# Attention and hard-swish feed-forward on one core: bias rows on Sync, later first weights, a fixed plan of feed-forward groups

## The chip, the cores and the metric

The kernel runs on one core of one Trainium2 chip. The core has five engines with queues of their own: TensorE (PE; its weight loads are listed as PEld), VectorE (DVE), ScalarE (ACT), GpSimd (POOL) and SyncE (SP). [...] DMA transfers are issued by SP, ACT or POOL and run on 16 DMA engines. The metric is the time of one execution on the device in microseconds (us), median over runs. A profile is one further execution; its times come from that execution.

## The reference

Attention over 8 batches of 8 heads, 576 positions, head dimension 64, with a selective bias from a running sum of `s`; the heads are then put side by side into rows of 512, and a feed-forward block with a hard-swish follows.

```python
scores = scale * np.matmul(q, k.transpose(0, 1, 3, 2))
cum = np.cumsum(np.maximum(s, 0.0), axis=-1)
bias = -(cum[:, :, :, None] - cum[:, :, None, :])
scores = np.where(causal, -1000000000.0, scores + np.minimum(bias, 0.0))
attn = np.exp(scores - max) ; attn = attn / (sum + 1e-09)
x = (attn @ v).transpose(0, 2, 1, 3).reshape(4608, 512)
h = x @ w_in                       # 512 x 2048
out = (h * np.clip(h + 3.0, 0.0, 6.0) / 6.0) @ w_out   # 2048 x 512
```

## The kernel before, in words

The 64 heads are worked on in 32 pairs, p = 0 to 31; four pairs make a batch. The work of a pair stands in one pass of a loop written out by hand: scores in three parts per head and a corner (line 277 on, `scores` and `corner`), exponentials on ScalarE (line 322), masks on VectorE (line 324), the product with v (`av`, line 373), the division (`norm`, lines 395 and 396) and the transposition of the result into `xT` (line 410 and 415, later by DMA). Each engine runs its instructions strictly in the order in which the program lists them. The "slots five to eight" of the change are p = 4 to 7.

Inputs come in three ways. `load_qk` (line 103) brings q and k of one pair: for the pairs 0 to 3 and from 9 on as float32 into one of three `raw` buffers by Sync, and `cast_qk` on GpSimd makes float16 tokens of them; for the pairs 4 to 8 (the ones that are not `flat`) GpSimd issues a transfer that casts on the way, into `tok`. `load_v` brings v by Sync in three transfers, and `cast_v` on GpSimd casts it. `load_aug` (line 135) copies the bias rows of a pair, 9 KB per head, from `rows_of` in SBUF into rows 64 to 67 of one of three `qk` buffers, in two transfers. In the first batch only these rows are needed there; from p = 5 on `set_stair` also copies a stair pattern into the rows 64 to 127, and the bias rows go over it. Scores of pair p read them. The first batch's rows come out of a short chain on VectorE (`cum1` to `cum6`, lines 602 to 630).

In a pair, `get(0)` and `get(1)` prepare the transposed q and k of the next pair: on TensorE up to pair 8, from the DMA-transposed `jt` afterwards.

The weights `w_in` come in four pieces of 1 MB (`load_w_in`) and `w_out` in eight of 0.5 MB (`load_w_out`), all issued by GpSimd with a cast to float16. GpSimd thus issues, in one queue and in program order, weights, the tokens of the pairs 4 to 8 and all bias rows.

The feed-forward work is cut into groups of four matmuls: `m1(n, ft)` makes 128 of the 2048 hidden columns for a block of 512 rows, followed by one ScalarE and one VectorE instruction (lines 454 and 455), in one of two PSUM banks `ph`; `m2(n, i)` adds a quarter of one output tile of 128 rows. 9 blocks of 16 and 16 make 288 groups. From p = 4 on eight places in each pair (seven at p = 4) call `group()`, which runs one m1 or one m2 or, in an alternation of the two, nothing. `m2_ready` holds an m2 back until enough m1 are done (LAG). After the last pair the remaining groups run back to back.

Of the kernel before, what the change touches and what calls it, by code (L numbers as in the profile page):

```python
# [18 lines left out]
def kernel(  # L19
# [10 lines left out]
    nc = tc.nc  # L30
# [7 lines left out]
    NP = NHEADS // 2  # L38
    PPB = H // 2
# [60 lines left out]
    def flat(p):  # L100
        return p < PPB or p >= NPE

    def load_qk(p, i, eng=nc.sync):
        b, h0 = p // PPB, 2 * (p % PPB)
        src = (q, k)[i][b, h0 : h0 + 2]
        if not flat(p):
            if not i:
                tok = work.tile([128, 24 * D], F16, tag="tok", bufs=4, name="tok")
                toks[p] = tok[0:96].rearrange("p (i h e d) -> p i h e d", i=2, h=2, e=6)
            nc.gpsimd.dma_start(  # L110
                out=toks[p][:, i].rearrange("p h e d -> p h (e d)"),
                in_=src.rearrange("h (p e) d -> p h (e d)", e=6),
            )
        else:
            eng.dma_start(
                out=raws[p % NRAW].rearrange("p (i t d) -> p i t d", i=2, t=9)[:, i],
                in_=src.rearrange("h s d -> (h s) d").rearrange(
                    "(t p) d -> p t d", p=128
                ),
            )  # L120

    def load_v(p, eng):
        b, h0 = p // PPB, 2 * (p % PPB)
        vraw = vraws[p % NRAW]
        for hh in range(2):
            eng.dma_start(
                out=vraw[:, hh, 0:4, :],
                in_=v[b, h0 + hh, 0:512, :].rearrange("(t p) d -> p t d", p=128),
            )
        eng.dma_start(  # L130
            out=vraw[0:64, :, 4, :],
            in_=v[b, h0 : h0 + 2, 512:SEQ, :].rearrange("h p d -> p h d"),
        )

    def load_aug(p, eng):
        for hh in range(2):
            g = 2 * p + hh
            eng.dma_start(  # L138
                out=qks[p % NQK][64:68, hh, :, 64 * hh : 64 * hh + SEQ],
                in_=rows_of[g // 32].rearrange("(r g) i t -> g r i t", g=32)[  # L140
                    g % 32, :, :, 0:SEQ
                ],
            )
# [315 lines left out]
    def m2(n, i):  # L459
        t4, fq = 2 * (i // 8) + i % 2, i % 8 // 2  # L460
        if fq == 0:
            po = psum.tile([128, 512], F32, tag="po", bufs=2, name="po")
            pos[n, t4] = po
        po = pos[n, t4]
        for ft in range(4 * fq, 4 * fq + 4):
            mm(  # L466
                po,
                lhsT=gTs[n][:, ft, t4 * 128 : (t4 + 1) * 128],
                rhs=w_out_sb[:, ft, :],
                start=(ft == 0),  # L470
                stop=(ft == NFT - 1),
            )
        if fq == 3:
            ob = work.tile([128, 512], F32, tag="ob", bufs=3, name="ob")
            nc.vector.tensor_scalar_mul(out=ob, in0=po, scalar1=1.0 / 6.0)  # L475
            r = n * 512 + t4 * 128
            nc.sync.dma_start(out=out[r : r + 128, :], in_=ob)
# [2 lines left out]
    m2_list = [(n, i) for n in range(NBLK) for i in range(16)]  # L480
    done = {1: 0, 2: 0}
    last = [2]
    tail = [False]
    LAG = 12

    def m1_ready():
        i = done[1]
        if i >= len(m1_list):
            return False
        return (512 * m1_list[i][0] + 511) // SEQ < x_done[0] // PPB  # L490

    def m2_ready():
        i = done[2]
        if i >= len(m2_list):
            return False
        n, j = m2_list[i]
        need = 16 * n + (4 * (j // 2) + 4 if j < 8 else 16)
        if done[1] == len(m1_list):
            return True
        return done[1] >= max(need + 2, i + LAG if n else 0)  # L500

    def group():
        a, c = m1_ready(), m2_ready()
        if not (a or c):
            return False
        if a and (last[0] == 2 or (tail[0] and not c)):
            m1(*m1_list[done[1]])
            done[1] += 1
            last[0] = 1
        else:  # L510
            if c:
                m2(*m2_list[done[2]])
                done[2] += 1
            last[0] = 2
        return True


    C = {}
# [8 lines left out]
    load_qk(0, 0)  # L527
    load_qk(0, 1, nc.scalar)
    nc.scalar.preload_act_table_set("natural_log_exp_and_others")
    for p in (1, 2):  # L530
        for i in range(2):
            load_qk(p, i)
        load_v(p - 1, nc.sync)
    for i in range(NROW):
        fill(nc.gpsimd, qks[i][64:68, :, :, :], 0.0)
    fill(nc.gpsimd, ident, 0.0)
# [105 lines left out]
    cum1(0, V)  # L642
    cum2(0)
    cast_qk(0, nc.scalar.copy)
    for i in range(2):
        load_qk(3, i)
    load_v(2, nc.sync)
    cum3(0, V)
    nc.scalar.copy(out=rows_of[0][0:32, 0, 0:SEQ], in_=C["c"][0:32])
    cum4(0, V)  # L650
# [5 lines left out]
    warm(NWARM[1])  # L656
    for g in range(1, 2 * NROW):
        pick(g)
    load_aug(1, nc.gpsimd)
    cast_qk(1)  # L660
    load_aug(2, nc.gpsimd)
    cast_v(0)
    cast_qk(2)
    load_w_in(0)
    cast_v(1)


    I, U = load_w_in, load_w_out
    weights_in = {
        2: ((I, 1),),  # L670
        3: ((I, 2),),
        4: ((I, 3), (U, 0), (U, 1)),
        5: ((U, 2), (U, 3)),
# [2 lines left out]
    }  # L676
    for p in range(NP):
        nxt = p + 1 < NP
        if p + 3 < NP:
            load_v(p + 3, nc.sync)  # L680
        if p == 1:
            nc.sync.dma_start(out=stair_sb, in_=stair_dram.ap())
        if NPE <= p + 4 < NP:
            for i in range(2):
                load_qk(p + 4, i)
        if PPB <= p < PPB + 3:
            set_stair((p + 1) % NQK, nc.gpsimd.tensor_copy)
            load_aug(p + 1, nc.gpsimd)
        c = p + 2
        if p and c < NP and flat(c):  # L690
            cast_qk(c)
            if c >= NPE:
                crossbar_qk(c)
        if p and nxt:
            cast_v(p + 1)
        if p and p < NP - 2 and not PPB <= p + 1 < PPB + 3:
            load_aug(p + 2, nc.gpsimd)
        for fn, c in weights_in.get(p, ()):
            fn(c)
        if p and PPB <= p + 3 < NPE:  # L700
            for i in range(2):
                load_qk(p + 3, i)
        if p == 10:
            load_s(1, (nc.sync,) * 4)
            fill(nc.gpsimd, rows_of[1][:, 0, :], 1.0)
        if p == 11:
            cum1(1, nc.gpsimd)
        if p == 12:
            cum2(1)
            nc.gpsimd.tensor_copy(out=rows_of[1][0:32, 0, 0:SEQ], in_=C["c"][0:32])  # L710
        if p == 13:
            cum3(1, nc.gpsimd)
            cum4(1, nc.gpsimd)
        if p == 13:
            cum5(1, nc.gpsimd)
            cum6(1, nc.gpsimd)

        def get(i):
            if p + 1 < NPE:
                transpose(p + 1, i)  # L720
            elif nxt:
                spread(p + 1, i)

        if p < PPB:
            scores(p, 0, 0)
            scores(p, 0, 1)
            get(0)
            scores(p, 0, 2)
            corner(p)
            if p:  # L730
                av(p - 1, 1, 0)
                av(p - 1, 1, 1)
                norm(p - 1, 1)
            get(1)
            scores(p, 1, 0)
            scores(p, 1, 1)
            if p:
                transpose_x(p - 1)
            av(p, 0, 0)
            scores(p, 1, 2)  # L740
            av(p, 0, 1)
            norm(p, 0)
            continue

        if p == PPB:
            early[0] = False
            scores(p, 0, 0)
            av(p - 1, 1, 0)
            m1_begin(0, 0, NKC - 1)
            av(p - 1, 1, 1)  # L750
            norm(p - 1, 1)
            scores(p, 0, 1)
            m1_begin(0, 1, NKC - 1)
            transpose_x(p - 1)
            group()
            group()
            scores(p, 0, 2)
            get(0)
            nc.vector.tensor_scalar(
                out=masks, in0=shut, scalar1=65504.0, scalar2=None, op0=ALU.add  # L760
            )
        else:
            scores(p, 0, 0)
            get(0)
            group()
            scores(p, 0, 1)
            av(p - 1, 1, 0)
            group()
            scores(p, 0, 2)
            av(p - 1, 1, 1)  # L770
            norm(p - 1, 1)
            group()
        corner(p)
        group()
        if p > NPE:
            x_done[0] = p - 1
        scores(p, 1, 0)
        get(1)
        group()
        scores(p, 1, 1)  # L780
        av(p, 0, 0)
        if p > PPB:
            (crossbar_x if p >= NPE else transpose_x)(p - 1)
        group()
        scores(p, 1, 2)
        group()
        av(p, 0, 1)
        norm(p, 0)
        group()
# [6 lines left out]
    group()  # L796
    group()
    transpose_x(p)
    tail[0] = True
    while group():  # L800
        pass
# [28 lines left out]
```

## Time and profile before

| | |
|---|---|
| median of 3 runs | 371.8 us (369.63 to 372.3) |
| the profiled execution | 370.86 us, its span 369.1 us |
| PE busy | 350.3 us (95%), 2886 matmuls |
| DVE, ACT, POOL busy | 245.3 us (66%), 220.1 us (60%), 130.5 us (35%) |
| Sync and POOL DMA queues (q1, q0) | 45.58 MB and 6.25 MB |
| one group of four matmuls | 0.864 us apart in the tail |
| tail after the last attention pair | about 75 us of groups |

A line of the profile names the engine, the source line, the operation and out<-in by the program's tile names. An x-count says how often; a releaser in brackets says what ended the idle time before it. The rows with 40 digits cut the span into equal slices and give the busy share in tenths. Landing is the time from the issue of a transfer until its semaphore has its full count.

### The profile page before, as it was taken

Reading aid. Unit: us, or ns where it says so; the run is one execution under the profiler, and the core shown is the slowest. Engines: PE = TensorE matmul, PEld = TensorE weight load, DVE = VectorE, ACT = ScalarE, POOL = GpSimd, SP = SyncE. Lnnn points to the kernel's source line nnn. Section 1 sums busy time; section 2 is a strip of 40 time slices with the busy share of each in tenths; the row PEclk is TensorE's granted clock in tenths of the full one; section 3 lists DMA queues with packets and bytes.
Section 4 is the critical chain, followed back from the end, with each engine's and each line's share of the span. In section 5 each row is a group of like instructions: output and inputs, shape, how many; then the busy total and the mean of one; then the engine's idle time right before and its main releaser. Section 6 shows DMA issues by size and latency. Waiting matters only on the chain.

```text
span 369.1 us, 7768 instructions
## 1 busy us (share of the span) xinstructions
PE 350.3 (95%) x2886; PEld 193.1 (52%) x2886; DVE 245.3 (66%) x551; ACT 220.1 (60%) x382; POOL 130.5 (35%) x227
## 2 busy tenths in 40 slices
PE   8969878979999999999999999999999999999995
PEld 3646544555555555555555555555555444444442
DVE  7654857777689977676767676767675644544531
ACT  4665765776667666666666666666666334334320
POOL 4959797433527733333333333333100000000000
PEclk9996999999999999999999999999999999999999
DMA  9999999999999596979797989696620101101111
GB/s 184 207 180 185 205 212 187 175 210 177 153 232 179 133 227 145 208 146 196 155 194 155 223 143 213 142 213 135 104 76 20 57 0 59 57 0 59 57 40 73
DMA packets 158261, 52.76 MB, mean 143 GB/s; under 512 B 146968, under 2 KB 153112, under 8 KB 158224
## 3 DMA queue, kind: packets, MB, share of 16 engines
q1 hardware_dynamic: 148608, 45.58, 62.0%
q0 software_dynamic: 8352, 6.25, 10.7%
q10 hardware_dynamic: 1264, 0.44, 0.6%
q8 instruction: 22, 0.36, 0.4%
q14 instruction: 15, 0.12, 0.1%
HBM read 37.36 MB, written 9.44 MB: 127 GB/s over the span
## 4 chain that ended last, share of the span: by engine, by line
PE 79%; DVE 6%; DMA 6%; POOL 4%; ACT 2%; issue 1%; SPq 1%; ACTq 0%; POOLq 0%; DVEq 0%
PE po L466 32%; PE ph L439 31%; PE O L373 6%; PE S L303 6%; DMA w_out_sb<-in_moe_w_out_dram 3%; PE S L292 3%; DMA vraw<-in_v_dram 2%; DVE gT L455 1%; POOL qk L138 1%; ACT tr L454 1%; DVE qk L206 1%; DVE P L324 1%; POOL tok L110 1%; DMA s_all<-in_s_dram 1%; ACT P L322 1%
## 5 line engine op out<-in xcount | busy, mean ns | idle before, releaser
L455 DVE SCALAR_TENSOR_TENSOR gT<-tr,ph 128x512 f16<-128x512 f32 x144 | 98.6, 685 | 85.0 <-ACT tr L454 83.9
L439 PE MATMUL ph<-xT,w_in_sb 128*128 128x512 f16 x576 | 148.2, 379 | 0.8 <-DVE xT L415 0.5
L466 PE MATMUL po<-w_out_sb,gT 128*128 128x512 f16 x576 | 146.3, 379 | 2.1 <-DVE x L396 1.4
L454 ACT ACTIVATE tr<-ph,bias 128x512 f32<-128x512 f32 x144 | 99.0, 687 | 79.4 <-PE ph L439 69.8
L322 ACT ACTIVATE P<-S 128x512 f16<-128x512 f32 x192 | 112.1, 594 | 49.6 <-PE S L292 24.5
L466 PEld LDWEIGHTS <-gT 128*128 128x128 f16 x576 | 49.8, 97 | 47.8 <-DVE x L396 1.5
L439 PEld LDWEIGHTS <-w_in_sb 128*128 128x128 f16 x576 | 51.5, 97 | 44.2 <-issue 0.4
L138 POOL DMA_DIRECT2D qk<-rows_of x62 | 36.0, 582 | 69.7 <-PE S L303 58.0
L303 PE MATMUL S<-qk 68*128 68x448 f16 (+3 forms) x256 | 49.8, 276 | 0.8 <-ACT P L322 0.8
L373 PE MATMUL O<-va,P 128*128 128x65 f16 x896 | 48.8, 195 | 1.7 <-DVE x L396 1.1
L373 PEld LDWEIGHTS <-P 128*128 128x128 f16 x896 | 40.4, 98 | 15.9 <-DVE x L396 1.6
L182 POOL CAST va<-vraw 128x512 f16<-128x512 f32 x32 | 19.8, 618 | 52.3 <-issue 28.8
L303 PEld LDWEIGHTS <-qk 68*128 68x128 f16 x256 | 24.0, 99 | 25.7 <-issue 1.7
L206 DVE COPY qk<-jt 64x768 f16<-64x768 f16 x92 | 34.4, 374 | 3.0 <-DMA jt<-tok 1.7
L178 POOL CAST tok<-raw 128x576 f16<-128x576 f32 x52 | 34.4, 687 | 2.7 <-DMA raw<-in_q_dram 1.3
L396 DVE TENSOR_TENSOR x<-O,rl 128x320 f16<-128x320 f32 x64 | 31.5, 492 | 2.2
L475 DVE TENSOR_SCALAR ob<-po 128x512 f32<-128x512 f32 x36 | 24.6, 684 | 7.0 <-PE po L466 7.0
L292 PEld LDWEIGHTS <-qk 128*128 128x128 f16 (+1 forms) x256 | 19.5, 98 | 17.0 <-issue 4.7
L324 DVE TENSOR_TENSOR P<-P,masks_sb 128x512 f16<-128x512 f16 x54 | 24.9, 462 | 4.1 <-ACT P L322 4.1
L292 PE MATMUL S<-qk 128*128 128x128 f16 (+1 forms) x256 | 25.3, 221 | 2.2 <-DMA qk<-rows_of 1.4
L395 DVE RECIPROCAL rl<-O 128x5 f32<-128x5 f32 x64 | 12.1, 189 | 5.9 <-PE O L373 5.8
L238 DVE COPY qk<-pt 64x576 f16<-64x576 f16 x12 | 9.6, 802 | 4.5 <-PE pt L228 4.4
(69 smaller groups left out, 166.7 us busy)
## 6 DMA issues: line engine op xcount, KB each, us to landing
out_dram<-ob SPq DMA_DIRECT2D x36, 256.0 KB, 2.1
vraw<-in_v_dram SPq DMA_DIRECT2D x64, 128.0 KB, 2.9
raw<-in_q_dram SPq DMA_DIRECT2D x27, 288.0 KB, 4.0
raw<-in_k_dram SPq DMA_DIRECT2D x26, 288.0 KB, 4.4
w_in_sb<-in_moe_w_in_dram POOLq DMA_DIRECT2D x4, 512.0 KB, 8.3
w_out_sb<-in_moe_w_out_dram POOLq DMA_DIRECT2D x8, 256.0 KB, 7.4
vraw<-in_v_dram SPq DMA_DIRECT2D x32, 32.0 KB, 2.9
qk<-rows_of POOLq DMA_DIRECT2D x62, 9.0 KB, 3.3
```

Of the source, the lines that this page charges most:

```text
L138: eng.dma_start(out=qks[p % NQK][64:68, hh, :, 64 * hh : 64 * hh + SEQ], in_=rows_of[g // 32].rearrange("(r g) i t -> g r i t", g=32)[g % ...
L178: copy(out=toks[p][:, c], in_=raws[p % NRAW][:, c])
L206: copies[par](out=qk[0:64, :, i, 128 * par : 128 * par + 256 * n].rearrange("p h (s two c) -> p h s two c", two=2, c=128)[:, :, :, 0, :], ...
L292: mm(S[:, c], lhsT=kT[rows, c], rhs=qT[rows, c], start=(j == 0 and not by_product), stop=(j == 3),)
L303: mm(S[:, c : c + w], lhsT=kT[0:68, 128 * j : 128 * (j + 1)], rhs=qT[0:68, 128 * (j + 1) : SEQ], start=(c == 0), stop=(c != 0 and p >= NROW),)
L322: nc.scalar.activation(out=pt[:, c], in_=S, func=AF.Exp, scale=0.125)
L373: mm(o[:, i, :], lhsT=lhsT, rhs=va[:, hh, j, 0:65], **kw)
L396: nc.vector.tensor_tensor(out=X[p][:, :, hh, :], in0=o[:, :, 0:64], in1=rl.to_broadcast([128, 5, 64]), op=ALU.mult,)
L439: mm(ph, lhsT=w_in_sb[:, kc, ft * 128 : (ft + 1) * 128], rhs=xT[:, kc, n * 512 : (n + 1) * 512], start=(kc == 0), stop=(kc == NKC - 1),)
L454: nc.scalar.activation(out=tr, in_=ph, func=AF.Relu, bias=bias3[:, 0:1])
L455: nc.vector.scalar_tensor_tensor(out=gTs[n][:, ft, :], in0=tr, scalar=6.0, in1=ph, op0=ALU.min, op1=ALU.mult)
L466: mm(po, lhsT=gTs[n][:, ft, t4 * 128 : (t4 + 1) * 128], rhs=w_out_sb[:, ft, :], start=(ft == 0), stop=(ft == NFT - 1),)
```

## The change

Four things are done together. The bias rows of the pairs 1 to 4 are issued by Sync, and the loads of the first pairs stand on Sync in the order: rows 1, q and k of 2, rows 2, v of 1, q and k of 3, v of 2; the rows 3 and 4 stand at the head of p = 1 and p = 2. The first piece of `w_in` is issued by GpSimd after the cast of q and k of pair 3, and the tokens of pair 4 right after the cast of pair 2. Within a pair, from p = 4 on, the loop lists the casts, then the weights, then the tokens of pair p + 3, and then the stair and the bias rows; and the float32 q and k are loaded three pairs ahead instead of four. `group()` takes its first 31 choices from a fixed plan (1 for m1, 2 for m2, a dot for nothing) for p = 4 to 7; after it a new rule with LAG 7 runs an m1 when no m2 is allowed.

```diff
-    tail = [False]
-    LAG = 12
+    LAG = 7
+    plan = list("1111.11" + "11.11.1." + "12.12.12" + "12122222")
...
-    def m2_ready():
+    def m2_ready(slack):
...
-        return done[1] >= max(need + 2, i + LAG if n else 0)
+        return done[1] >= need + slack and (not slack or done[1] >= i + LAG)
...
     def group():
-        a, c = m1_ready(), m2_ready()
-        if not (a or c):
-            return False
-        if a and (last[0] == 2 or (tail[0] and not c)):
+        if plan:
+            what = plan.pop(0)
+            a, c = what == "1", what == "2"
+        else:
+            a, c = m1_ready(), m2_ready(2)
+            if not a and not c:
+                c = m2_ready(0)
+        if a and (last[0] == 2 or not c):
             m1(*m1_list[done[1]])
             done[1] += 1
             last[0] = 1
-        else:
-            if c:
-                m2(*m2_list[done[2]])
-                done[2] += 1
+        elif c:
+            m2(*m2_list[done[2]])
+            done[2] += 1
             last[0] = 2
-        return True
+        return a or c
...
-    for p in (1, 2):
-        for i in range(2):
-            load_qk(p, i)
-        load_v(p - 1, nc.sync)
+    for i in range(2):
+        load_qk(1, i)
+    load_v(0, nc.sync)
...
     cast_qk(0, nc.scalar.copy)
-    for i in range(2):
-        load_qk(3, i)
-    load_v(2, nc.sync)
...
-    load_aug(1, nc.gpsimd)
+    load_aug(1, nc.sync)
+    for i in range(2):
+        load_qk(2, i)
+    load_aug(2, nc.sync)
+    load_v(1, nc.sync)
+    for i in range(2):
+        load_qk(3, i)
+    load_v(2, nc.sync)
     cast_qk(1)
-    load_aug(2, nc.gpsimd)
     cast_v(0)
     cast_qk(2)
-    load_w_in(0)
-    cast_v(1)
+    for i in range(2):
+        load_qk(4, i)
...
     weights_in = {
-        2: ((I, 1),),
         3: ((I, 2),),
...
     for p in range(NP):
         nxt = p + 1 < NP
+        if 0 < p < PPB - 1:
+            load_aug(p + 2, nc.sync)
+        if NPE <= p + 3 < NP:
+            for i in range(2):
+                load_qk(p + 3, i)
+        c = p + 2
+        if p == 1:
+            cast_v(1)
+            cast_qk(3)
+        elif p == 2:
+            load_w_in(0)
+            cast_v(2)
+            cast_v(3)
+            load_w_in(1)
+        elif p:
+            if NPE <= c < NP:
+                cast_qk(c)
+                crossbar_qk(c)
+            if nxt:
+                cast_v(p + 1)
+            for fn, c in weights_in.get(p, ()):
+                fn(c)
         if p + 3 < NP:
             load_v(p + 3, nc.sync)
-        if p == 1:
+        if p == 2:
             nc.sync.dma_start(out=stair_sb, in_=stair_dram.ap())
-        if NPE <= p + 4 < NP:
+        if 2 <= p and PPB < p + 3 < NPE:
             for i in range(2):
-                load_qk(p + 4, i)
+                load_qk(p + 3, i)
         if PPB <= p < PPB + 3:
             set_stair((p + 1) % NQK, nc.gpsimd.tensor_copy)
             load_aug(p + 1, nc.gpsimd)
-        c = p + 2
-        if p and c < NP and flat(c):
-            cast_qk(c)
-            if c >= NPE:
-                crossbar_qk(c)
-        if p and nxt:
-            cast_v(p + 1)
-        if p and p < NP - 2 and not PPB <= p + 1 < PPB + 3:
+        if p > PPB + 1 and p < NP - 2:
             load_aug(p + 2, nc.gpsimd)
-        for fn, c in weights_in.get(p, ()):
-            fn(c)
-        if p and PPB <= p + 3 < NPE:
-            for i in range(2):
-                load_qk(p + 3, i)
```

More of the change, by code (lines that the diff above doesn't have):

```diff
@@ L499, in m2_ready @@
             return True
-        return done[1] >= max(need + 2, i + LAG if n else 0)
+        return done[1] >= need + slack and (not slack or done[1] >= i + LAG)
     def group():
-        a, c = m1_ready(), m2_ready()
-        if not (a or c):
-            return False
-        if a and (last[0] == 2 or (tail[0] and not c)):
+        if plan:
+            what = plan.pop(0)
+            a, c = what == "1", what == "2"
+            assert not a or m1_ready()
+            assert not c or m2_ready(0)
+        else:
[3 more added lines that the diff above has]
+        if a and (last[0] == 2 or not c):
             m1(*m1_list[done[1]])
@@ L798 @@
     transpose_x(p)
-    tail[0] = True
     while group():
```

## The prediction
> **What bounds the kernel now.** I read the 40 slices first: after slice 13 (120 us) TensorE is full to the last slice, so only the first third holds time. The DMA row, read as the mean share of 16 engines, is full over just that third.
>
> ```profile
> PE   8969878979999999999999999999999999999995
> PEclk9996999999999999999999999999999999999999
> DMA  9999999999999596979797989696620101101111
> ```
>
> Then the waits of TensorE, and windows of 10 us (PE, PEld, DVE, ACT, POOL busy; granted clock, DMA share, GB/s).
>
> ```profile
> PE pt L228 <- DMA tok<-in_q_dram: 2.3, 1, 2.3
> PE S L292 <- DMA qk<-rows_of: 1.4, 1, 1.4
> PE O L373 <- POOL va L182: 0.6, 1, 0.6
> ...
> 20.00:30.00 10.00, 5.74 (x82) 4.33 (x80) 4.42 (x11) 4.54 (x10) 7.37 (x14) 0.87 0.97 181
> 30.00:40.00 10.00, 9.01 (x106) 6.54 (x104) 5.06 (x12) 6.92 (x13) 9.32 (x14) 0.79 1.20 187
> ```
>
> The reader is to see that the stalls in p=2 and p=3 are deliveries: v of pair 2, bias rows of pair 3, tokens of pair 4. The clocks 0.87 and 0.79 mean 2.6+4.2 = 6.8 us at half rate; the 5.6 us of TensorE work in them cost 2.8 us extra.
>
> From the timeline of TensorE I took the first score of each pair: p=0 9.34, p=4 34.07, p=5 43.15, p=9 79.08, p=14 121.84. An undisturbed pair of the first batch takes 4.10 (15.00 to 19.10). In the steady part a pair takes 9.22 with eight groups 0.864 apart (the spacing in the tail), so attention is 2.31; PE transposes add 0.78 in p=5 to 7 and 0.28 in p=8. Against these sums the losses are: p=0 to 3, 24.7-16.4 = 8.3; p=4 (four groups), 9.08-6.54 = 2.5; p=5 to 13 (53 groups), 78.7-69.2 = 9.5. From p=14 on there is none.
>
> Last the POOL timeline around p=4, where the bias rows of p=5 stand:
>
> ```profile
> 30.68 0.80 POOL L146 DMA_DIRECT2D w_in_sb<-in_moe_w_in_dram  x1
> 31.42 0.68 POOL L110 DMA_DIRECT2D tok<-in_q_dram  x1
> 32.06 0.69 POOL L110 DMA_DIRECT2D tok<-in_k_dram  x1
> 32.79 2.45 POOL L562 COPY qk<-stair_sb 64x1280 f16<-64x1280 f16 x2
> 35.18 1.18 POOL L138 DMA_DIRECT2D qk<-rows_of  x2
> 36.40 0.61 POOL L182 CAST va<-vraw 128x512 f16<-128x512 f32 x1
> 36.95 0.29 POOL L183 CAST va<-vraw 64x128 f16<-64x128 f32 x1
> 37.19 0.78 POOL L146 DMA_DIRECT2D w_in_sb<-in_moe_w_in_dram  x1
> 37.97 1.44 POOL L154 DMA_DIRECT2D w_out_sb<-in_moe_w_out_dram  x2
> 41.06 0.65 POOL L110 DMA_DIRECT2D tok<-in_q_dram  x1 [1.66 <-DMA w_in_sb<-in_moe_w_in_dram]
> ```
>
> A 9 KB bias transfer issued at 35.2 lands 7.8 us later, at 43.0; p=5 opens at 43.15. It had queued behind the POOL transfers ahead of it.
>
> **The Trainium skill.** "DMA: Bandwidth & Descriptors", section "Queues, rings and completion order", says that each DMA engine takes its queues in turn a packet at a time and each ring in order. The trace agrees: POOL's landings follow issue order, and Sync's v for p=6, issued at 30.6 to 31.9 beside POOL's weights, took 8.6 to 11.0 us, against 4.0 to 4.3 for v issued at 26.5. Its section "Issuing engines are not separate DMA queues" says that a change of issuer saves only issue time; so moving bias rows to Sync adds no bandwidth. "TensorE: Matmul & The Clock Gate", Part 1, says that an idle window of about 3.4 us halves the clock until a busy one has passed; here the half clock followed the stalls of p=3.
>
> **The change, part by part.** No instruction of TensorE is added or removed except in order, so the time moves by TensorE's losses alone.
>
> *Bias rows 1 to 4 on Sync.* Eight issues of about 0.6 us (the shortest Sync rows are 0.58 to 0.61) leave POOL and enter Sync, in front of q and k of pair 2, v of 1, q and k of 3, v of 2. Sync now stands until the rows are ready (line 630 ends at 8.60), so q of pair 2 goes out near 9.8 instead of 7.88. Landing took 4.0 and 5.1: q 14, k 15.5. TensorE wants them at 15.1 and 16.4 after a cast of 0.67: covered, by under 0.3 for k. POOL starts its first cast 1.3 us earlier, which removes the 0.55 wait at 11.36. A Sync bias landing is not shown; POOL's took 2.1 to 4.8, I take 3. Pair 1 needs it by 14.6: no cost to 0.5.
>
> *w_in(0) behind the casts.* Its 512 KB no longer stand (15.0 to 22.2) before k, v and tokens. Tokens of p=4 are issued at 15.3 instead of 24.6. k of pair 3 now ends last, about 20.5, cast 21.2 against 20.5 wanted: 0.8; v of pair 2: 0.5; bias rows of pair 3 land at 23.5, wanted at 24.7. So p=4 opens at 15.00 (p=1 before) -0.55+3x4.10+1.3 = 28.05, with 0.75 for waits too small to list 28.8: **5.3 earlier**, and no half clock there.
>
> *POOL's order in p=4.* The loop now puts the stair copies and the bias rows of p=5 behind w_in(3), w_out(0), w_out(1) and the tokens of p=7. Landings of before in that queue price it: w_in(1) 35.4, tokens(5) 37.3, w_in(2) 40.8, tokens(6) 42.9, bias(5) 43.2, w_in(3) 46.2, w_out(1) 49.7, tokens(7) 51.8, w_out(3) 55.7, tokens(8) 57.7. A pair of token loads takes 2.0, 1 MB of weights 3.0 to 5.1, mean 3.8. New chain: w_in(0) is issued at 21.2 and lands near 27.5 (7.2 before, beside a full Sync queue); w_in(1) 31.3, tokens(5) 33.3, w_in(2) 37.1, tokens(6) 39.1; w_in(3) waits on POOL for the cast of v of p=5, which Sync delivers at about 37.7 through the weights, 1.5 lost; w_in(3) 44.4, w_out(1) 48.2, tokens(7) 50.2, **bias(5) 50.5**. Weights at 3.0 and no gap give 45; at 5 with a gap 55.
>
> *What TensorE does meanwhile.* p=4 with six groups: 3.09+5.18 from 28.8, 2 for tokens(5), 0.5 for xT: ready for p=5 at 39.6. The scores of p=5 read the bias rows and everything on TensorE stands behind them: 11 us idle. p=5 opens at 50.5 against 43.15, +7.35, with two groups more done, -1.73: **+5.6**. What is queued behind the rows (tokens of 8, rows of 6 near 58) is then in time: p=6 opens near 61.5.
>
> *p=5 to 13.* Losses after: half clock following 11 us of idle, 2.3 (bounds 1.7 to 3.4 by the page and by 2.8 here); p=5 with five first-layer groups, where VectorE has 8.6 us of work against 7.4, 1.5; p=6 to 13, 3.2, since p=8 now has eight groups instead of one (it lost 2.0) and w_out is in. 7.0 against 9.5: **-2.5**.
>
> *Runs of first-layer groups.* LAG 7 and the new rule give, from p=13, "....1111 11121211 21211121 21222222" with period four, where before 1 and 2 alternated. Two ph banks: a group's bank is free after ScalarE and VectorE, and 1, 1, 1 comes back to it after 2x0.864+2x0.45 = 2.6 us or less.
>
> ```profile
> 195.39 0.69 ACT L454 ACTIVATE tr<-ph,bias 128x512 f32<-128x512 f32 x1 [0.27 <-PE ph L439]
> 196.11 0.69 DVE L455 SCALAR_TENSOR_TENSOR gT<-tr,ph 128x512 f16<-128x512 f32 x1 [1.50 <-ACT tr L454]
> ```
>
> Group end to ACT 0.2, ACT to DVE 0.72, DVE to free 0.74: 1.7 after the group's 0.864, 2.5 without any queueing. Walking a run of seven with exps (0.58 apart) and masks, norms and spreads in line gives stalls of 0.21, 0.18, 0.21, 0, 0.23: 0.8 per run, five runs, plus 0.15 on each "111": **+4.2** (0 if the queues slip favourably, 8 if a late jt transfer stands in a run).
>
> *Sum.* +5.6-2.5+4.2 = +7.3 on the profiled 370.86 (span 369.1 and 1.8 around it), which lies 0.9 under the median 371.8; on the median 379.
>
> **Rivals.** (a) *The order of need wins.* The rows of p=5 come before TensorE is ready, because weights move at 3 us per MB or faster once Sync's loads are earlier and the queue started without a gap. p=5 opens at 39.6: -3.5-1.7; p=5 to 13 then lose 4.7, -4.8; runs +4.2: -5.8, **366**. For it: before was limited by exactly these deliveries. Against it: 11 us of transfers now stand ahead. It turns at a landing of 43.2, where the sum is zero. (b) *Rows late, runs free*: TensorE's other waits absorb them, +3.1, **375**. (c) *Longer chain*: Sync's v starves behind weights, POOL stands in casts, rows of p=5 near 56 and those of p=6 late too, **386**. That the plan is not followed is excluded: it is fixed at build, and the new order shows on TensorE.
>
> **Numbers.** Main case 0.48 at 379 (376 to 383), (a) 0.20, 361 to 368, (b) 0.20, 373 to 377, (c) 0.12, 383 to 390. Faster by over 1% (under 368.1) 0.17; within 1% (about what a measurement of this kernel tells from no change) 0.18; slower (over 375.5) 0.65. Range 366 to 387 leaves out part of (a) and (c).
>
> **What would show it.** Scores at line 292's place in p=5 waiting about 11 us on "qk<-rows_of", the clock halved after it; p=4 opening near 29; no wait on tokens of p=4; from p=14 small waits of ph on gT. I am wrong if p=5 opens before 43, or if ph never waits.

## The result, and the profile after

The changed kernel takes 389.88 us (median of 4 runs, 386.88 to 390.87) against 371.87: **slower, ratio 1.048, 95% interval 1.041 to 1.056**. Its profiled execution (390.87 us, the longest of the four) has a span of 389.1 us, 20.0 more than the profiled one of before; the medians lie 18.0 apart.

The 40 slices of the changed kernel (one is 9.7 us, counted from 0) show two dips of TensorE where before had shallower ones or none: slices 2 to 5, and slices 13 and 14.

```profile
PE   8968568999999879999999999999999999999995
PEclk9988859999999989999999999999999999999999
```

Its waits of TensorE (total, times, longest; `po` is the bank of a second-layer group, `gT` what VectorE makes of a first-layer group for the second layer), and as the last line the only wait on gT of before, where the bias rows cost 1.4 in all:

```profile
PE S L292 <- DMA qk<-rows_of: 10.2, 2, 7.8
PE ph L439 <- DVE gT L455: 6.9, 9, 2.5
PE po L466 <- DVE gT L455: 3.4, 6, 0.9
...
PE ph L439 <- DVE gT L455: 0.2, 1, 0.2
```

TensorE's timeline puts places to them (start, duration; in brackets the idle time before and what ended it). The first line is the opening of p=5 in the kernel before, the others are of the changed kernel:

```profile
43.15 0.38 PE L292 MATMUL S<-qk 128*128 128x128 f16 x4
...
26.71 0.58 PE L292 MATMUL S<-qk 68*128 68x128 f16 x4 [2.38 <-DMA qk<-rows_of]
...
51.88 0.58 PE L292 MATMUL S<-qk 128*128 128x128 f16 x4 [7.79 <-DMA qk<-rows_of]
...
138.32 1.74 PE L439 MATMUL ph<-xT,w_in_sb 128*128 128x512 f16 x4 [2.48 <-DVE gT L455]
...
165.45 0.39 PE L466 MATMUL po<-w_out_sb,gT 128*128 128x512 f16 x1 [0.42 <-DVE gT L455]
...
184.85 1.02 PE L439 MATMUL ph<-xT,w_in_sb 128*128 128x512 f16 x4 [0.92 <-DVE gT L455]
```

The line at 51.88 is the opening of p=5, the one at 26.71 the opening of p=3. The first-layer wait at 138.32 lies in p=13, the last two in the part that lost next to nothing before. POOL's timeline in p=4 answers to the one shown of before:

```profile
38.00 0.61 POOL L182 CAST va<-vraw 128x512 f16<-128x512 f32 x1 [6.70 <-DMA vraw<-in_v_dram]
...
39.14 0.77 POOL L146 DMA_DIRECT2D w_in_sb<-in_moe_w_in_dram  x1 [0.17 <-issue]
39.89 1.42 POOL L154 DMA_DIRECT2D w_out_sb<-in_moe_w_out_dram  x2
...
42.64 2.46 POOL L566 COPY qk<-stair_sb 64x1280 f16<-64x1280 f16 x2
45.03 1.21 POOL L138 DMA_DIRECT2D qk<-rows_of  x2
```

POOL stands 6.70 us for the v of p=5, then issues weights and tokens, and gets to the bias rows at 45.0 (35.2 before). They land 6.7 us later, at 51.7; TensorE had been ready at 44.1.

The openings of the pairs split the 20.0. p=5 opens 8.73 later (51.88 against 43.15) with two groups more done (1.73): **+7.0**. p=5 to 13 lose 13.0 against 9.5: **+3.5**, of which p=13 alone is 4.3 (5.3 lost against 1.0). From p=14 to the end, groups counted: **+9.5**.

The first of these numbers varies from execution to execution. The version "old rule" of experiment 1 below is the same program up to p=8, and in its profile p=3 waits for no bias rows, p=4 opens at 29.24 instead of 33.08, and p=5 opens at

```profile
50.46 0.58 PE L292 MATMUL S<-qk 128*128 128x128 f16 x4 [10.33 <-DMA qk<-rows_of]
```

which makes +5.6 in place of +7.0. So differences of a us or two before p=5, between single profiles, carry no argument.

### The profile page after: what moved, and what is told of

Its sections match the earlier page's. It is cut to its first block, busy times and chain, and to the rows that moved or that the text cites. A ratio compares the mean times of both kernels' runs of the same rounds, so it can differ in the third digit from the quotient of the medians.

```text
span 389.1 us, 7712 instructions
## 1 busy us (share of the span) xinstructions
PE 357.4 (92%) x2886; PEld 195.3 (50%) x2886; DVE 252.4 (65%) x551; ACT 219.2 (56%) x382; POOL 129.1 (33%) x219
## 4 chain that ended last, share of the span: by engine, by line
PE 69%; DVE 11%; DMA 9%; ACT 5%; issue 2%; POOL 2%; SPq 2%; POOLq 0%
PE po L466 30%; PE ph L439 26%; PE O L373 5%; PE S L303 5%; DVE gT L455 4%; ACT tr L454 3%; DMA qk<-rows_of 3%; DMA vraw<-in_v_dram 3%; DMA raw<-in_q_dram 3%; PE S L292 3%; DVE qk L206 2%; DVE P L324 2%; DVE x L396 1%; ACT P L322 1%; ACT qk L238 1%
## 5 line engine op out<-in xcount | busy, mean ns | idle before, releaser
L439 PE MATMUL ph<-xT,w_in_sb 128*128 128x512 f16 x576 | 150.9, 384 | 8.2 <-DVE gT L455 6.9
L466 PEld LDWEIGHTS <-gT 128*128 128x128 f16 x576 | 50.6, 97 | 51.4 <-DVE gT L455 6.3
L178 POOL CAST tok<-raw 128x576 f16<-128x576 f32 x52 | 35.9, 692 | 62.3 <-DMA raw<-in_q_dram 48.1
L138 POOL DMA_DIRECT2D qk<-rows_of x54 | 31.9, 591 | 63.6 <-PE S L303 54.8
L303 PE MATMUL S<-qk 68*128 68x448 f16 (+3 forms) x256 | 50.3, 278 | 0.2 <-ACT P L322 0.2
L206 DVE COPY qk<-jt 64x768 f16<-64x768 f16 x92 | 36.9, 401 | 1.1
L324 DVE TENSOR_TENSOR P<-P,masks_sb 128x512 f16<-128x512 f16 x54 | 26.3, 488 | 16.4 <-ACT P L322 16.4
L352 ACT ACTIVATE PC<-Sc 128x128 f16<-128x128 f32 x32 | 8.8, 275 | 7.3 <-PE Sc L344 7.3
```

Of the source, the lines that this page charges most:

```text
L178: copy(out=toks[p][:, c], in_=raws[p % NRAW][:, c])
L206: copies[par](out=qk[0:64, :, i, 128 * par : 128 * par + 256 * n].rearrange("p h (s two c) -> p h s two c", two=2, c=128)[:, :, :, 0, :], ...
L303: mm(S[:, c : c + w], lhsT=kT[0:68, 128 * j : 128 * (j + 1)], rhs=qT[0:68, 128 * (j + 1) : SEQ], start=(c == 0), stop=(c != 0 and p >= NROW),)
L324: nc.vector.tensor_tensor(out=pt[:, c], in0=pt[:, c], in1=masks[:, c], op=ALU.min)
L439: mm(ph, lhsT=w_in_sb[:, kc, ft * 128 : (ft + 1) * 128], rhs=xT[:, kc, n * 512 : (n + 1) * 512], start=(kc == 0), stop=(kc == NKC - 1),)
L466: mm(po, lhsT=gTs[n][:, ft, t4 * 128 : (t4 + 1) * 128], rhs=w_out_sb[:, ft, :], start=(ft == 0), stop=(ft == NFT - 1),)
```

## The experiments

Each ratio is against the kernel before on the same chip.

**1. Rows and rule, one taken back at a time.** The first version puts stair and bias rows ahead of the weights again; the second goes back to the old choice of groups after the plan (`alternate` holds the `group` and `m2_ready` of before, with LAG 12); the third does both.

```diff
+        if PPB <= p < PPB + 3:
+            set_stair((p + 1) % NQK, nc.gpsimd.tensor_copy)
+            load_aug(p + 1, nc.gpsimd)
         c = p + 2
...
-        if PPB <= p < PPB + 3:
-            set_stair((p + 1) % NQK, nc.gpsimd.tensor_copy)
-            load_aug(p + 1, nc.gpsimd)
```

```diff
         else:
-            a, c = m1_ready(), m2_ready(2)
-            if not a and not c:
-                c = m2_ready(0)
+            return alternate()
```

Rows first:

> Only the place of the stair copies and of the bias rows of p=5, 6 and 7 in GpSimd's queue is changed: they stand ahead of the casts, weights and tokens of the pair before, as they did before the change. Queue theory: p=5 opens when TensorE is ready for it, near 44 us instead of 51.9, and the half clock that follows the 7.8 us stall goes too (p=5 lost 3.0 us): 8 to 10 us faster than the changed kernel, 380 to 382 us. Rival (late start of the weights is what makes the rows late, not the order): the rows still land after 49 us and less than 3 us come back.

Old rule:

> The fixed plan stays for p=4 to 7; after it the choice of groups is the one of before (LAG 12, strict alternation of the two layers). Theory of runs: from p=14 no TensorE wait of ph or po on gT is left (9.5 us), p=11 and p=13 lose about 1 us instead of 6.7, p=8 loses 1.2 more: about 13 us faster than the changed kernel, 376 to 378 us. Rival (late deliveries: q and k are loaded three pairs ahead instead of four, and GpSimd waits 60 us for them, so the transposed q and k reach VectorE late): the waits stay and less than 4 us come back.

Both:

> The two edits rows_first and old_rule together. If their causes are separate the gains add: 389.9 - 9 - 13 = 368 us (365 to 371), which is under the kernel before. If the stall at p=5 had hidden something that comes next (first layer at p=5 and 6 waiting for the third and fourth piece of w_in, or w_out), the sum is short by that much: 372 to 376 us.

| | new rule | old rule |
|---|---|---|
| rows behind the weights | 389.88 (the changed kernel) | 377.09, ratio 1.0145 (1.0094 to 1.0197) |
| rows ahead of the weights | 380.16, ratio 1.0237 (1.0173 to 1.0302) | **370.19**, ratio 0.9951 (0.9931 to 0.9971) |

All three came out within what was expected of them. Taken from the changed kernel, the rows' place is worth 9.7 and the rule 12.8. Together they are worth 19.7, not 22.5, so 2.8 of the two losses overlap; what overlaps was not taken apart. What is left is a version 0.5% faster than the kernel before. The longest of its waits of TensorE is 1.8:

```profile
PE ph L439 <- DVE gT L455: 2.8, 3, 1.8
```

**2. Each part alone, put into the kernel before.** The rows' issues are moved to the end of the tokens' loads with nothing else changed, or the new rule (`group_new`, with the changed kernel's `m2_ready` and LAG 7) is used from p=8 on with nothing else changed.

```diff
-        if PPB <= p < PPB + 3:
-            set_stair((p + 1) % NQK, nc.gpsimd.tensor_copy)
-            load_aug(p + 1, nc.gpsimd)
         c = p + 2
...
                 load_qk(p + 3, i)
+        if PPB <= p < PPB + 3:
+            set_stair((p + 1) % NQK, nc.gpsimd.tensor_copy)
+            load_aug(p + 1, nc.gpsimd)
```

> The kernel before with one edit: in p=4 to 6 the stair copies and the two bias-row transfers of the next pair are issued on POOL behind that pair's weights and tokens instead of ahead of them. Theory (position alone makes the late rows): the rows of p=5 queue behind w_in(3), w_out(0), w_out(1) and the tokens of p=7, some 2 MB more; they land near 51 to 52 instead of 43.0, p=5 opens there, and the kernel takes 378 to 382. Rival (the late start of the weight queue, w_in(0) behind the casts, makes them late): the rows land near 45 to 46 and the time is 373 to 375.

```diff
     def group():
+        if p >= 2 * PPB:
+            return group_new()
```

> The kernel before with only the choice of groups changed from p=8 on: the changed kernel's rule (LAG 7, first-layer groups in runs, second-layer groups with no slack where nothing else is ready). Theory (the rule costs by itself, on any start): slower by what it cost in the changed kernel, 9 to 14, so 381 to 385, with waits of ph and po on gT in every block of four pairs. Rival (the rule costs only because the first third shifted the blocks against the pairs): under 4, so 372 to 375.

Rows late alone: 381.09, ratio 1.026 (1.021 to 1.032). In POOL's timeline the first of the two transfers goes out at 39.97, behind the weights:

```profile
33.15 0.80 POOL L146 DMA_DIRECT2D w_in_sb<-in_moe_w_in_dram  x1
...
39.97 0.60 POOL L138 DMA_DIRECT2D qk<-rows_of  x1 [0.58 <-POOL qk L562]
```

and TensorE's timeline shows what waited for it:

```profile
50.62 0.59 PE L292 MATMUL S<-qk 128*128 128x128 f16 x4 [8.62 <-DMA qk<-rows_of]
```

p=5 opens at 50.62, within the 50.46 to 51.88 of the two profiles with the changed kernel's beginning. So the place in the queue makes the lateness, and no share of the late start of the weights, the rival, can be seen. "DMA: Bandwidth & Descriptors" of the Trainium skill, section "Queues, rings and completion order", says, where it deals with the queues of SP and ACT, that a DMA engine takes descriptors in ring order. GpSimd's queue agrees here: the landings follow the order of issue, and the 9 KB issued at 39.97 landed at 50.5, 10.5 us later, just after the 2 MB of weights and the tokens ahead of it (the last at 50.3).

Rule alone: 380.68, ratio 1.024 (1.020 to 1.028), 0.3 under the range expected and far from the rival's 372 to 375. A block of four pairs (p=18 to 21) takes 38.36 us in it, 36.89 before. Its timeline of TensorE holds the 1.5 between them. The last product with v (`PC`) is followed by a first-layer group in a run, and later by a group for which nothing has to be waited:

```profile
171.04 0.19 PE L373 MATMUL O<-va,PC 128*128 128x65 f16 x1
171.28 1.02 PE L439 MATMUL ph<-xT,w_in_sb 128*128 128x512 f16 x4
...
184.61 0.20 PE L373 MATMUL O<-va,PC 128*128 128x65 f16 x1
184.64 1.02 PE L466 MATMUL po<-w_out_sb,gT 128*128 128x512 f16 x4
```

The group starts 0.24 after the product in the one place and 0.03 in the other. Five such delays of first-layer groups (0.15, 0.21, 0.15, 0.28, 0.10; each too short for the list of waits) make 0.9 a block, and one second-layer group taken with no slack, at 195.19, makes 0.58.

**3. What in the rule costs.** The rule takes a second-layer group with no slack (right after the last first-layer group that it reads, without two more in between) where nothing else is ready, so that these run out early and first-layer groups then come in runs ("....1111 11121211 21211121 21222222 22221111" from p=13). On the version with the rows ahead (380.16), that clause is left out, or LAG is 12 with the clause kept:

```diff
             a, c = m1_ready(), m2_ready(2)
-            if not a and not c:
-                c = m2_ready(0)
```

> The version that takes 380.2 (the changed kernel with stair and bias rows ahead of the weights on POOL), without the last clause of the new choice of groups: a second-layer group is no longer taken with no slack where nothing else is ready, the slot stays empty. The order is then 21 21 21 21 with one 22 and one 11 in four pairs, no runs; LAG stays 7. Theory (the runs and the slack-0 groups are the whole cost of the rule): 370 to 372, no waits of ph on gT from p=14. Rival (a second-layer group seven behind its first layer, LAG 7, costs by itself): 374 to 378.

```diff
-    LAG = 7
+    LAG = 12
```

> The version that takes 380.2 with LAG 12 in place of 7 and the slack-0 clause kept: first-layer groups now come twelve in a row in p=13 and 14, second-layer groups eleven in a row. Theory (each first-layer group beyond the second in a run can wait for one of two ph banks): more groups in runs, so slower, 382 to 387, with more waits of ph on gT. Rival (the slack-0 groups cost it, and there are as many or fewer of them): 377 to 381.

Without the clause: 374.23, ratio 1.0072 (1.0048 to 1.0096), inside the rival's 374 to 378 at its lower edge, and 2.2 above the theory's range. The time alone would thus speak for the rival, that LAG 7 costs by itself; the trace speaks against it. From p=14 there is no wait on gT, and blocks of four pairs take 36.89, as before. So LAG 7 costs nothing there, and the clause is the whole loss of that part. In the profiles, what keeps this version above the one with both edits lies in p=12 and 13, which lose 3.2 each (0.5 and 1.9 there). Slots stay empty in them, and TensorE waits for exponentials, masks and spreads (VectorE's copies of `jt` into `qk`), up to 1.0 at a time. Whether LAG 7 or the missing clause empties them was not tried apart.

With LAG 12: 381.88, ratio 1.0275 (1.0232 to 1.0317), just under the 382 to 387 of the theory and above the rival's range; its interval overlaps that of the version with LAG 7 (1.0173 to 1.0302), so that it is slower is not shown. Its waits of TensorE:

```profile
PE ph L439 <- DVE gT L455: 9.9, 17, 1.9
```

No wait of po on gT is left (3.5 with LAG 7), while ph waits 17 times (10 times, 6.7 us, with LAG 7). Longer runs thus trade one wait for the other, at about the same sum.

**4. Loads three or four pairs ahead.**

```diff
-        if NPE <= p + 3 < NP:
+        if NPE <= p + 4 < NP:
             for i in range(2):
-                load_qk(p + 3, i)
+                load_qk(p + 4, i)
```

In the changed kernel:

> Only the float32 loads of q and k are put back to four pairs ahead, in the same place of the loop. Theory of runs: GpSimd's 60 us of waiting for raw q and k go, TensorE's waits do not: within 1 us of the changed kernel, 389 to 391 us. Rival of late deliveries: 4 to 9 us faster, 381 to 386 us.

In the version that takes 370.2:

> The version that takes 370.2 with the float q and k of each pair from p=9 on loaded four pairs ahead, as before, not three. Theory (worth the 1.8 that it was worth in the changed kernel): 368 to 369. Rival (the 1.8 came from buffers next to the late rows or the runs): 369.7 to 370.7.

In the changed kernel 388.06, ratio 1.044 (1.041 to 1.048): 1.8 less, more than expected, but within the spread of the changed kernel's own runs (386.88 to 390.87), so the times don't show the gain; the length of the blocks below does. POOL had waited 22 times, 48 us in all, for the raw q in the changed kernel, and its casts then came in the middle of VectorE's spreads. In POOL's timeline of the changed kernel:

```profile
131.95 1.27 POOL L625 TENSOR_TENSOR r<-c,rows_of 64x576 f32<-64x576 f32 x1
...
134.11 1.28 POOL L634 TENSOR_TENSOR rows_of<-r,rows_of 32x576 f16<-32x576 f32 x1
...
182.08 0.66 POOL L178 CAST tok<-raw 128x576 f16<-128x576 f32 x1 [2.56 <-DMA raw<-in_q_dram]
```

and in VectorE's, at the same places; the last line is of the kernel before with the rule alone, where no cast stands beside the spreads:

```profile
132.07 1.43 DVE L324 TENSOR_TENSOR P<-P,masks_sb 128x512 f16<-128x512 f16 x1
133.43 2.11 DVE L206 COPY qk<-jt 64x768 f16<-64x768 f16 x2
...
137.60 1.26 DVE L455 SCALAR_TENSOR_TENSOR gT<-tr,ph 128x512 f16<-128x512 f32 x2
...
182.94 1.14 DVE L206 COPY qk<-jt 64x768 f16<-64x768 f16 x2
184.11 1.28 DVE L455 SCALAR_TENSOR_TENSOR gT<-tr,ph 128x512 f16<-128x512 f32 x2
...
178.69 0.65 DVE L206 COPY qk<-jt 64x768 f16<-64x768 f16 x2
```

A pair of spreads takes 0.65 where POOL does not cast beside it and 1.02 to 1.14 where it does: 8 of 31 such pairs between 140 and 290 us in the changed kernel, none of 31 with four ahead, one of 30 before. The two gT instructions behind the spreads at 182.94 are what the ph wait at 184.85 ends on. With four ahead, blocks of four pairs take 38.4, as in the kernel before with the rule alone; in the changed kernel 38.75 to 39.2. So of about 2.1 per block 1.5 is the order of the groups, and the other 0.6 goes with POOL beside VectorE. Why an overlap slows them, "SBUF — State Buffer" of the skill says in "SBUF: two separate sides": VectorE (in some of its modes) and GpSimd share one pair of ports, and whichever comes second blocks. The lengthening agrees with it; no run here tested the port by itself.

In the version that takes 370.2 the same edit cost time: 372.72, ratio 1.0028 (1.0007 to 1.0049), both expectations missed. That version has alternating groups and slow spreads too (10 of 30), at no cost to TensorE: its blocks take 36.89. In the profile with four ahead p=6 takes 12.96 instead of 9.78 after a p=5 that is 1.6 shorter, and TensorE waits 3.3 us in all for spreads (1.0 without the edit), nearly all of it where p=13 and 14 open. That the first of these loads, now issued in the crowded p=5, does this is a guess, and was not tried apart.

**5. The rest of the change.** Sync's order in p=1 and 2 (the bias rows of pair 3 ahead of v of pair 3), and the fixed plan left out, both on the version that takes 370.2:

```diff
+        if 0 < p < 3:
+            load_v(p + 2, nc.sync)
-        if p + 3 < NP:
+        if 2 <= p and p + 3 < NP:
             load_v(p + 3, nc.sync)
```

> The version that takes 370.2 (bias rows and stair ahead of the weights on POOL, old choice of groups after the plan), with the Sync queue of p=1 and p=2 reordered: bias rows of pair 3 ahead of v of pair 3. Theory (pair 3's wait of 2.4 and the half clock after it carry through to the end): p=4 opens 3 to 5 earlier, near 29, and the time is 365 to 368. Rival (p=5 is held by its own delivery near 43 whatever p=4 does): p=4 opens earlier, p=5 does not, 369.5 to 371.

```diff
-    plan = list("1111.11" + "11.11.1." + "12.12.12" + "12122222")
+    plan = []
```

> The version that takes 370.2 without the fixed plan: groups of p=4 to 7 by the old alternation. Theory (the two groups more that the plan puts into p=4 are done while TensorE would wait for the rows of p=5): p=5 opens at the same 43 with two groups fewer done, 371.5 to 372.5. Rival (the plan only moves groups): within 0.7 of 370.2.

Rows of pair 3 earlier: 370.39, ratio 0.9972 (0.9951 to 0.9992), no gain. p=4 opens at 29.1 instead of 32.5 ("old rule" had 29.24 without this edit), and then waits for what comes next:

```profile
34.64 0.48 PE L228 MATMUL pt<-ident,tok 96*128 96x96 f16 x6 [1.39 <-DMA tok<-in_q_dram]
...
42.44 0.38 PE L292 MATMUL S<-qk 128*128 128x128 f16 x4 [0.52 <-DMA qk<-rows_of]
```

Of 3.3 us at p=4, 0.7 are left at p=5 (43.18 before this edit). The rival was right: p=5 is held by its own delivery. With q and k four ahead as well the version took 373.39, ratio 1.0044 (1.0021 to 1.0067), slower than either number of this expectation:

> The version with pair 3's rows ahead of its v on Sync (370.4), and q and k four pairs ahead. Theory (both edits add): 367.5 to 369. Rival (neither reaches the end): 370 to 371.

Without the plan: 373.47, ratio 1.0061 (1.0035 to 1.0088). p=5 opens at 42.56 after a wait of 2.0 with two groups fewer done, as the theory had it; the loss of 3.3 is larger than its 1.3 to 2.3, and what makes the rest was not found. The plan earns its place: it fills TensorE while p=5's rows are on their way.

## Why the prediction was wrong

The direction was right (slower, 379 against 389.9), and the time fell beyond the range of 366 to 387.

*Rows of p=5 late, +5.6: right, measured +7.0.* The rows landed at 51.7 where the chain of landings gave 50.5, behind the very transfers named. In this profile two steps inside were off. p=4 opened at 33.1, not 28.8: the bias rows of pair 3 were taken to land at 23.5, but Sync issued them only at 21.3, behind the three transfers of v of pair 3, and they landed near 26.6. TensorE was therefore ready at 44.1 instead of 39.6 and stood 7.8 instead of 11 us. In the profile of "old rule" both came out nearly as forecast, though Sync issued the rows at 21.4 there too: p=4 opened at 29.24, and TensorE was ready at 40.1 and stood 10.3. The landing of the rows of pair 3 thus varies, and the forecast left that out; experiment 5 shows that p=5's own wait hides it.

*p=5 to 13, -2.5: measured +3.5.* p=5 lost 3.0, half clock after the stall (forecast 3.8 with the VectorE work); the windows of the changed kernel (PE, PEld, DVE, ACT, POOL busy; granted clock, DMA share, GB/s) show the clock:

```profile
40.00:50.00 10.00, 3.78 (x31) 1.81 (x29) 4.90 (x9) 3.96 (x8) 9.58 (x14) 0.82 1.12 179
50.00:60.00 10.00, 8.12 (x66) 4.71 (x67) 4.86 (x10) 4.75 (x9) 6.27 (x10) 0.67 1.23 214
```

What "TensorE: Matmul & The Clock Gate", Part 1, says of an idle window of about 3.4 us, that it halves the clock, is borne out: the wait that ends at 51.88 is followed by a granted clock of 0.67. (The forecast's bounds of 1.7 to 3.4 for this are an estimate from that window.) p=6 to 12 lost 4.7, where 3.2 was allowed up to 13. The rest is p=13 alone, 5.3. Its first four slots stay empty, as they do before; in the others stand four first-layer groups where before the two layers alternate, and VectorE, with masks and spreads lengthened by POOL's bias chain, falls behind until 137.6. The clock then halves once more: from 138.5 to 141.9 us it is 0.50, and the two groups at 138.32 and 140.25 take 1.74 and 1.83 instead of 1.02. From the spacing of the instructions that is an estimated 1.6 of the 5.3. No single wait of 3.4 us stands before it; TensorE was busy for 1.0 of the 3.5 us from 135.0. Not all of p=13 is the rule's: with the old rule p=13 loses 3.4 behind late rows and 1.9 without, against 1.0 before. The sum took no account of p=13, although the order of groups that it quoted, "....1111", shows it.

*Runs of first-layer groups, +4.2: this is the step that failed; measured +9.5 from p=14, and 4.3 more in p=13.* The rule is worth 9.1 by itself (experiment 2, against the 371.55 of the kernel before on that chip) and 12.8 beside the late rows. The mechanism, one of two ph banks coming back too late, was right, and so was the size of what was walked: 0.8 a run and 0.15 for a "111" were forecast, and in the kernel before with the rule alone the first-layer groups lose 0.9 a block. The step that failed is that the term held nothing else. It left out the second-layer groups taken with no slack, which wait for the gT of the group just before (0.42 to 0.9, six times); the lengthening of VectorE's spreads to 1.02 to 1.14 beside POOL's casts, since the walk gave them the durations of an undisturbed pair (some 0.6 a block); and p=13. The upper bound of 8 given for this term was too low for the same reasons.

*The rivals.* (a), the order of need wins, at 366: refuted for this kernel, since the rows land 8.5 us after the turning point of 43.2; with the rows taken out of the chain and the old rule the rest of the change is worth 0.5% (0.3 to 0.7). (b), runs free, at 375: refuted by experiments 1 and 2. (c), longer chain, 386: nearest in time, and in part in cause. POOL did stand 6.7 us in the cast of v, where 1.5 was forecast, but the rows still landed at 51.7 and not at 56: the queue ahead of that cast was still busy, with the tokens of p=6 landing at 40.0, and the transfers behind it stayed near the forecast: w_in(3) landed at 45.9 (44.4 forecast), the tokens of p=7 at 51.5 (50.2).

*Signs that were named.* The wait of the scores of p=5 on the bias rows, the half clock after it, no wait on tokens of p=4 and the waits of ph on gT from p=14 are all there. p=4 near 29 is not in this profile, but is in that of "old rule".

## What to carry to other kernels

A small transfer that many instructions stand behind has to be priced by its place in its queue: 9 KB put behind 2 MB cost 9.5 us here, with nothing else changed (experiment 2). A rule that never leaves a slot empty is not free: it uses up the groups that keep two kinds alternating, and the runs that follow expose the two-bank chain from TensorE over ScalarE and VectorE and back, and the groups pulled forward wait themselves; look at the whole period of the order, both kinds of group and the empty slots included, before pricing one run. And when such a run is walked, let the VectorE instructions have the durations they show beside GpSimd's work, not their best ones. Last, take a second profile of the same beginning before explaining a us in it: here p=4 opened at 33.08 in one and at 29.24 in another.

## What was not expected of the hardware

The same pair of VectorE copies (64x768, float16) took 0.65 us alone and 1.02 to 1.14 beside a GpSimd cast, and up to 2.11 beside GpSimd's bias chain; the same overlap cost TensorE nothing from p=14 on where groups alternated, and showed in its waits where they came in runs.

The clock also halved without a wait as long as the 3.4 us window that the page on TensorE gives: in the version with both edits it is 0.50 from 48.9 to 52.3 us, where the longest wait before was 1.8 and TensorE had been busy for 1.6 of the 3.4 us from 45.5.
